# A score unit's two products issued back to back, and the fillers moved between the units

## The chip, the core and the metric

The kernel runs on one NeuronCore of a Trainium2 chip. Its engines are TensorE (PE, with its weight loads shown apart as PEld), VectorE (DVE), ScalarE (ACT), GpSimd (POOL) and SyncE (SP, which here issues nearly all DMAs). The metric is the device time of one execution in microseconds (us). Shown before: a median of 1024.78 us over 3 runs (1022.85 to 1027.67).

## What is computed

One transformer block on a sequence of S = 2048 rows of width D = 512, in fp32. Cut to the part that matters here, the attention reads:

```
q, k, v = x @ wq, x @ wk, x @ wv        # 32 heads of 16, 4 segments of 512 rows
logits = einsum("bhqd,bhkd->bhqk", qs, ks) * scale + mask     # per segment and head, causal
p      = softmax(logits, axis=-1)
a_dot  = einsum("bhqk,bhkd->bhqd", p, vs)
o      = g * a_mem + (1.0 - g) * a_dot   # a_mem: a linear memory of the earlier segments
x      = x + ga * (o @ wo)               # then layer norm, a GELU feed-forward of 1792, residual
```

The softmax needs, for each head and query row, the maximum of its 512 masked logits. Four segments times 32 heads make 128 independent 512x512 score blocks.

## The kernel before, in words

The program has three stages: projections (until about 177 us), attention (about 177 to 714 us) and the feed-forward. The change touches the attention stage alone.

**Units.** Heads are taken four at a time: Q counts 0 to 31 (a "turn" below is the work of one Q), P = 2Q and 2Q + 1 are its two pairs of heads, and h (0 or 1) is the head within a pair. The two heads of a pair lie in different halves of the array's rows, so that a product of h = 0 and one of h = 1 may run side by side. For every head there are two sorts of unit, each in three sizes:

- A score unit S (`s_unit`, products on line 622) computes logits with queries on the partitions, only to find row maxima. Size a is the block of the last 128 queries (512 keys), b the next (384), and **c holds two blocks, of 256 and of 128 keys**. The maxima are taken by a VectorE instruction on line 610 (`masked_max`), one for each block, straight from PSUM.
- A transposed unit T (`t_unit`, products on line 681) computes the logits again with keys on the partitions and the maximum already subtracted: two more rows of the stacked operands `qst` hold it. ScalarE exponentiates it into `pta`, `ptb` or `ptc` (line 684), and GpSimd zeroes what is above the diagonal (line 666).

Score units run four pairs of heads ahead of transposed ones (`LEAD`). Both take their PSUM bank from a rotation of six, `bank("att")`, so the seventh allocation has to wait until the first bank has been read.

**Fillers.** Other products stand between the units:

- Read-outs and their way back (`m_rows`, `m_put`, `m_send`): GpSimd gathers the maxima of a Q, `m_put` transposes them by one product (line 639), ScalarE copies them to `ms`, and SP writes them into two rows of `qst` for the T units of that Q.
- Value products (`pv_part`, line 702): four parts j = 0 to 3 per Q, of 512, 384, 256 and 128 columns, into the single bank `pv`, which `pv_out` copies out after the last.
- Output parts (`wo_part`, line 790): three full-width products into the bank `mm`, two such triples in a turn once the first segment is done.
- `v_last` (line 466): value projections of the last segment, done in the first turns.

**What sets the order.** The string `ORDER` lists the units of one turn, with 20 slots c0 to c19 between them. The table `PRM` gives each filler a position: `20 * Q + d` is slot d of turn Q (d of 20 or more lies in a later turn). Each engine executes what is put on it strictly in that order; semaphores that the framework derives from the tiles do the rest. It keeps a PSUM bank as a whole: a product into a bank waits for a reader of another part of it.

Of the kernel before, what the change touches and what calls it, by code (L numbers as in the profile page):

```python
# [22 lines left out]
VW = 17  # L23
VROW = 576
EPS = 1e-5
ORDER = ('Sa0 Ta1 c0 Ta0 Sa1 c1 c2 Sb0 Tb1 c3 Tb0 Sb1 c4 c5 Sc0 Tc1 c6 Tc0 Sc1 c7 '
         'Sa2 Ta3 c8 c9 Ta2 Sa3 c10 c11 Sb2 Tb3 c12 Tb2 Sb3 c13 Sc2 Tc3 c14 Tc2 Sc3 c15 c16 c17 c18 c19')
PRM = {'turn': 2,
 'pv': [[31, 0, 0, 512], [36, 1, 128, 512], [37, 2, 256, 512], [38, 3, 384, 512]],
 'pvlast': [[25, 0, 0, 512], [30, 1, 128, 512], [31, 3, 384, 512], [35, 2, 256, 512]],  # L30
 'mrows': -21,
 'mput': [-16, -15],
 'stacks': -65,
 'den': 95,
 'dnl': 18,
 'rbl': 13,
# [7 lines left out]
 'olo': 138,  # L44
 'quick': {'dnl': 11, 'den': 84, 'rbl': 12, 'mix': 107, 'ohi': 117, 'olo': 119},
 'end': {'dnl': 11, 'den': 84, 'rbl': 7, 'mix': 103, 'ohi': 111, 'olo': 116},
 'wo': [[20 * i + o for i in range(8) for o in (4, 11)]] * 2 + [[20 * i + o for i in range(4) for o in (4, 7, 11, 18)]],
 'wox': -25,
 'mixu': 12,
 'olou': 12,  # L50
# [4 lines left out]
 'wl': [26, 66, 77, 81],  # L55
 'gate': 209,
# [45 lines left out]
def block_kernel(ctx: ExitStack, tc: tile.TileContext, x, wq, wk, wv, wo, betaq, betam,  # L102
# [22 lines left out]
    def copy(e, dst, src):  # L125
        if e == "a":
            act.activation(dst, src, AF.Copy)  # L127
        else:
            (v if e == "v" else pool).tensor_copy(dst, src)
# [74 lines left out]
    with ExitStack() as pa:  # L204
# [4 lines left out]
        def pst(name):  # L209
            return pp.tile([128, 512], F32, tag="ps", name=name)  # L210
# [107 lines left out]
        ps = pst("mpsa")  # L318
# [10 lines left out]
        for ds in ((0,), (1, 2, 3)):  # L329
# [4 lines left out]
            n = slice(ds[0], ds[-1] + 1)  # L334
# [177 lines left out]
        for s in range(NSEG):  # L512
            for tok in PRM["A"][s].split():
                n = int(tok[1]) if len(tok) > 1 and tok[1].isdigit() else 0
                if tok[0] in "QKN":
                    proj(s, "k" if tok[0] == "K" else "q", n)
                elif tok[0] == "V":
                    ps = pst(f"v{s}_{n}")
# [64 lines left out]
    with ExitStack() as pb:  # L583
# [17 lines left out]
        def bank(n):  # L601
            turn[n] = turn.get(n, -1) + 1
            return banks[n][turn[n] % len(banks[n])]
# [4 lines left out]
        def masked_max(dst, src, n):  # L608
            n_dump[0] += 1
            v.tensor_tensor_reduce(out=dump[n_dump[0] % 2][:, :n], in0=src, in1=maskb[:, 512 - n:], scale=-1.0, scalar=-4 * NEG,  # L610
                                   op0=ALU.add, op1=ALU.min, accum_out=dst)

        def s_unit(P, z, h):
            Q, p = P // 2, P % 2
            if Q not in nms:
                nms[Q] = nmt[Q % len(nmt)]
            ps = bank("att")
            o = 0
            for i in ((3,), (2,), (1, 0))["abc".index(z)]:
                n = 128 * (i + 1)  # L620
                q, k = stack(qst, P, h, 48), stack(kst, P, h, 48)
                pe.matmul(ps[:, o:o + n], q[:, 128 * i:128 * i + 128], k[:, :n], start=True, stop=True)  # L622
                masked_max(nms[Q][:, h, p, i:i + 1], ps[:, o:o + n], n)
                o += n

        def stack(st, P, h, rows):
            return st[P // 2 % NK][64 * h:64 * h + rows, P % 2].bitcast(F32R)
# [7 lines left out]
            nss[Q] = r  # L635

        def m_put(Q):
            ps = bank("pv")
            pe.matmul(ps[:, :128], nss.pop(Q), identr, start=True, stop=True)
            ms = sb.tile([32, 128], F32, tag="ms", bufs=2, name=f"ms{Q}")  # L640
            copy(PRM["mse"], ms, ps[:32, :128])
            mss[Q] = ms
# [232 lines left out]
        def at(P, part, f, *a):  # L875
            todo.setdefault((P, part), []).append((f, a))
# [23 lines left out]
        def ap(pos, f, *a):  # L900
            at(pos // 10, pos % 10, f, *a)
# [8 lines left out]
        for Q in range(32):  # L910
            z = Q // 8
            pv = PRM["pv" if Q < 31 else "pvlast"]
            pvo = pv[3][0]
            ap(20 * Q + PRM["mrows"], m_rows, Q)
            put = 20 * Q + PRM["mput"][Q < 2]
            ap(put, own, "pv", ("m", Q), m_put, (Q,), True)
            ap(put + PRM["msl"], m_send, Q)
            for i, (d, j, lo, hi) in enumerate(pv):
                ap(20 * Q + d, own, "pv", Q, pv_part, (Q, j, lo, hi, i == 0, i == 3), False)
            ap(20 * Q + pvo, own, "pv", Q, pv_out, (Q,), True)  # L920
            if Q < 31:
                ap(20 * Q + pvo + PRM["tsl"], pv_store, Q)
# [60 lines left out]
        for Q in range(-LEAD // 2, NP // 2 + 1):  # L983
            for k, P in enumerate(PRM["w1at"]):
                if P // 2 == Q:
                    load_w1(k)
            for tok in ORDER.split():
                if tok[0] == "c":
                    n = int(tok[1:])
# [19 lines left out]
    with ExitStack() as pc:  # L1009
        c1 = pc.enter_context(tc.tile_pool(name="c1", bufs=1, side="right", reuse_waits="tile"))  # L1010
# [255 lines left out]
        for p in range(2):  # L1266
            n = FH * p + FH - 1
# [56 lines left out]
        for p in range(2):  # L1324
            for j in range(FH):
                quad(FH * p + j, j == 0)
            n = FH * p + FH - 1
# [73 lines left out]
```

## Time and profile before

| what | value |
|---|---|
| runs shown | 1027.67, 1024.78, 1022.85 us |
| profiled execution: its own time, its span | 1025.51 us, 1023.8 us |
| mean granted TensorE clock over the span | 0.813 |
| busy PE, DVE, ACT, POOL | 920.7, 577.9, 453.1, 279.9 us |
| granted clock from 213 to 392 us, 392 to 614 us, 614 to 695 us | 0.56, 0.62, 0.81 |

Durations in the trace are those of one execution. A busy PE is modelled: a product counts as busy until its result has drained, so consecutive products overlap in the list. The granted clock is a separate record; in the attention stage it takes the values 0.5 and 1.0 alone, for stretches of 3.41 us or a multiple. "Idle before, releaser" names what ended an engine's wait.

### The profile page before, as it was taken

The page shows a single profiled execution, that of the slowest core. Times are in us where ns is not written, and L with a number is a line of the kernel's source. Part 1 is how long each engine was busy: PE and PEld are TensorE (multiplying, and loading weights), DVE is VectorE, ACT ScalarE, POOL GpSimd, SP SyncE. Part 2 cuts the span into 40 slices and gives each one's busy share as a digit, 9 for nine tenths or more (in the row PEclk, how much of TensorE's full clock was granted, in tenths as well). Part 3 has the DMA queues.
Part 4 walks back from the last instruction along what each step waited for, and adds up shares of the span by engine and source line. Part 5 has one row for each costly group of instructions (what it writes and reads, how often), then busy time and mean ns, then how long its engine had stood idle before and what let it go on. Part 6 is the DMA issues. An engine that isn't in the chain of part 4 may idle for free.

```text
span 1023.8 us, 14348 instructions
## 1 busy us (share of the span) xinstructions
PE 920.7 (90%) x4521; PEld 600.4 (59%) x4521; DVE 577.9 (56%) x1624; ACT 453.1 (44%) x882; POOL 279.9 (27%) x503
## 2 busy tenths in 40 slices
PE   9999999878887888878887888779999999999998
PEld 5877786543333344334333344335788888888887
DVE  6676754454555554455545545558878597543243
ACT  4444445134444344343433344436667544465221
POOL 1232421022343323323332463425232003221000
PEclk9999999755565555666665658878999999999999
DMA  8957639323334345344543354743485756454543
GB/s 291 346 198 282 225 132 318 104 43 93 87 94 106 75 105 107 92 99 112 130 111 98 102 123 109 163 140 107 145 287 197 236 180 181 134 176 144 177 144 110
DMA packets 102707, 156.23 MB, mean 153 GB/s; under 512 B 15332, under 2 KB 31076, under 8 KB 102632
## 3 DMA queue, kind: packets, MB, share of 16 engines
q1 hardware_dynamic: 101768, 153.76, 50.1%
q10 hardware_dynamic: 864, 1.57, 0.4%
q8 instruction: 35, 0.57, 0.2%
q14 instruction: 40, 0.33, 0.1%
HBM read 93.95 MB, written 60.83 MB: 151 GB/s over the span
## 4 chain that ended last, share of the span: by engine, by line
PE 74%; DVE 10%; issue 9%; POOL 2%; DMA 2%; ACT 2%; SPq 0%; DVEq 0%; ACTq 0%
PE att L622 11%; PE pv L702 9%; PE bx L1048 7%; DVE dump L610 7%; PE att L681 5%; PE mm L790 5%; PE bx L1318 4%; PE q L315 4%; PE by L1318 4%; PE bv L1318 4%; PE bv L1048 4%; PE k L315 3%; PE v L466 3%; PE spare L1318 2%; PE by L1048 2%
## 5 line engine op out<-in xcount | busy, mean ns | idle before, releaser
L610 DVE CUSTOM_DVE_ANT_0 dump<-att,maskb 128x512 bf16<-128x512 f32 (+3 forms) x512 | 236.9, 489 | 246.9 <-PE att L622 130.2
L622 PE MATMUL att<-kst,qst 48*128 48x512 f32 (+3 forms) x512 | 216.4, 501 | 87.6 <-DVE nm L610 87.6
L622 PEld LDWEIGHTS att<-kst,qst 48*128 48x128 f32 x512 | 117.9, 262 | 182.2 <-DVE nm L610 121.4
L681 PE MATMUL att<-qst,kst 50*128 50x512 f32 (+3 forms) x512 | 165.9, 487 | 8.2 <-DVE nm L610 7.6
L684 ACT ACTIVATE pta<-att 128x512 f32<-128x512 f32 x128 | 69.4, 595 | 102.3 <-PE pv L702 48.5
L681 PEld LDWEIGHTS att<-qst,kst 50*128 50x128 f32 x512 | 89.0, 265 | 27.8 <-DVE nm L610 23.3
L684 ACT ACTIVATE ptc<-att 128x384 f32<-128x384 f32 x128 | 55.9, 488 | 90.6 <-PE att L681 73.8
L666 POOL TENSOR_SCALAR_AFFINE_SELECT ptc<-ptc 128x256 f32<-128x256 f32 x128 | 51.5, 413 | 95.9 <-ACT ptc L684 91.4
L666 POOL TENSOR_SCALAR_AFFINE_SELECT pta<-pta 128x256 f32<-128x256 f32 x64 | 27.5, 429 | 176.5 <-ACT pta L684 171.9
L684 ACT ACTIVATE ptb<-att 128x384 f32<-128x384 f32 x128 | 57.5, 499 | 16.8 <-PE att L681 10.5
L834 POOL TENSOR_TENSOR wb<-wa 128x256 f32<-128x256 f32 x24 | 20.2, 843 | 152.1 <-DVE hr L855 68.0
L702 PE MATMUL pv<-pta,V 128*32 128x512 f32 x248 | 56.5, 1002 | 0.0
L127 ACT ACTIVATE ts<-pv 128x512 f32<-128x512 f32 x31 | 18.6, 599 | 77.8 <-PE pv L702 72.0
L136 DVE TENSOR_TENSOR gl<-s,gh 128x512 fp32r<-128x512 f32 x34 | 24.1, 709 | 41.9 <-ACT gh L133 41.8
L702 PEld LDWEIGHTS pv<-ptc,V 128*32 128x32 f32 x496 | 24.0, 170 | 38.1 <-issue 37.6
L702 PE MATMUL pv<-ptc,V 128*32 128x256 f32 (+1 forms) x496 | 45.1, 512 | 0.0
L702 PE MATMUL pv<-ptb,V 128*32 128x384 f32 x248 | 43.4, 790 | 0.0
L610 DVE DVE_READ_ACCUMULATOR2_ANT nm<- 128x1 f32 x512 | 42.4, 83 | 0.0
L133 ACT ACTIVATE gh<-s 128x512 fp32r<-128x512 f32 x34 | 21.3, 628 | 46.6 <-PE spare L1318 17.2
L1053 ACT ACTIVATE s<-s,b1t 128x512 f32<-128x512 f32 x42 | 30.3, 721 | 21.1 <-DVE s L1057 21.1
L1057 DVE TENSOR_TENSOR s<-bv,s 128x512 f32<-128x512 f32 x28 | 19.3, 688 | 31.5 <-PE bv L1048 21.9
L666 POOL TENSOR_SCALAR_AFFINE_SELECT ptb<-ptb 128x256 f32<-128x256 f32 x64 | 26.2, 409 | 38.1 <-ACT ptb L684 38.0
(363 smaller groups left out, 2083.1 us busy)
## 6 DMA issues: line engine op xcount, KB each, us to landing
GD<-s SPq DMA_DIRECT2D x56, 256.0 KB
s<-GD SPq DMA_DIRECT2D x52, 256.0 KB
kst<-KD SPq DMA_DIRECT2D x64, 192.0 KB
qst<-QD SPq DMA_DIRECT2D x64, 192.0 KB
QD<-q SPq DMA_DIRECT2D x16, 512.0 KB
KD<-k SPq DMA_DIRECT2D x16, 512.0 KB
TD<-ts SPq DMA_DIRECT2D x32, 256.0 KB
xt<-X2D SPq DMA_DIRECT2D x28, 256.0 KB
```

Source lines behind the costliest of these rows:

```text
L315: pe.matmul(ps, a[:, k, 128 * g:128 * g + 128], b[k], start=(k == 0 and i == 0), stop=(k == KB - 1 and i == 2))
L466: pe.matmul(ps, a[k][:, 128 * b:128 * b + 128], w[:, k, :], start=(k == 0 and i == 0), stop=(k == KB - 1 and i == 2))
L610: v.tensor_tensor_reduce(out=dump[n_dump[0] % 2][:, :n], in0=src, in1=maskb[:, 512 - n:], scale=-1.0, scalar=-4 * NEG, op0=ALU.add, op1=AL ...
L622: pe.matmul(ps[:, o:o + n], q[:, 128 * i:128 * i + 128], k[:, :n], start=True, stop=True)
L666: pool.affine_select(out=t, in_=t, pattern=pattern, compare_op=ALU.is_ge, fill=0.0, base=0, channel_multiplier=-1)
L681: pe.matmul(ps[:, o:o + n], k[:, 128 * j:128 * j + 128], q[:, 128 * j:], start=True, stop=True)
L684: act.activation(pt[:, h, :], ps[:, :m], AF.Exp, scale=0.25)
L702: pe.matmul(ps[32 * c:32 * c + 32, lo:hi], V[4 * s + j][:, VW * hd:VW * hd + 32], pt[:, c % 2, lo - o:hi - o], start=start, stop=stop)
L790: pe.matmul(ps, a[:, 128 * b:128 * b + 128], w[:, g, :], start=(g == 0 and i == 0), stop=(g == 3 and i == 2))
L1048: pe.matmul(ps, a[:, i, k, :], b[k], start=start and k == 0 and c == 0, stop=k == 1 and c == 2, skip_group_check=not start)
L1053: act.activation(dst, src, AF.Gelu_apprx_tanh, bias=b1t[:, f:f + 1])
L1318: pe.matmul(ps, a[:, c], w[:, lo:hi], start=(f == 0 and i == 0), stop=(last and i == 2))
```

## The change

Three things change, all in the attention stage.

1. In `s_unit`, the products of a unit are issued first, and then its maxima. Only size c has more than one.
2. `m_put` takes its bank from the rotation of six rather than the `pv` bank, and its slot goes from 4 (5 for the first two Q) to 6 of the turn.
3. Positions: the four value products of a Q go from 31, 36, 37 and 38 to 21, 27, 30 and 35; an output triple goes from slot 11 to slot 13 (the last segment here: 4, 7, 11, 18 to 4, 9, 13, 17); the stack loads go from -65 to -63; the sixteen steps of `v_last` get even distances. In `ORDER` slot c8 now stands ahead of Sa2, c14 ahead of Sc2, and c16 between Tc3 and Tc2.

```diff
-ORDER = ('Sa0 Ta1 c0 Ta0 Sa1 c1 c2 Sb0 Tb1 c3 Tb0 Sb1 c4 c5 Sc0 Tc1 c6 Tc0 Sc1 c7 '
-         'Sa2 Ta3 c8 c9 Ta2 Sa3 c10 c11 Sb2 Tb3 c12 Tb2 Sb3 c13 Sc2 Tc3 c14 Tc2 Sc3 c15 c16 c17 c18 c19')
+ORDER = ('Sa0 Ta1 c0 Ta0 Sa1 c1 c2 Sb0 Tb1 c3 Tb0 Sb1 c4 c5 Sc0 Tc1 c6 Tc0 Sc1 c7 c8 '
+         'Sa2 Ta3 c9 Ta2 Sa3 c10 c11 Sb2 Tb3 c12 Tb2 Sb3 c13 c14 Sc2 Tc3 c15 c16 Tc2 Sc3 c17 c18 c19')
- 'pv': [[31, 0, 0, 512], [36, 1, 128, 512], [37, 2, 256, 512], [38, 3, 384, 512]],
+ 'pv': [[21, 0, 0, 512], [27, 1, 128, 512], [30, 2, 256, 512], [35, 3, 384, 512]],
- 'mput': [-16, -15],
- 'stacks': -65,
+ 'mput': [-14, -14],
+ 'stacks': -63,
- 'wo': [[20 * i + o for i in range(8) for o in (4, 11)]] * 2 + [[20 * i + o for i in range(4) for o in (4, 7, 11, 18)]],
+ 'wo': [[20 * i + o for i in range(8) for o in (4, 13)]] * 2 + [[20 * i + o for i in range(4) for o in (4, 9, 13, 17)]],
- 'vl': [[-39, -36, -39, -36], [-31, -31, -27, -23], [-19, -18, -19, -18], [-9, -9, -4, -1]],
+ 'vl': [[-39, -37, -36, -34], [-33, -31, -29, -28], [-26, -24, -22, -20], [-18, -13, -8, -3]],
...
-            o = 0
+            o, parts = 0, []
             for i in ((3,), (2,), (1, 0))["abc".index(z)]:
                 n = 128 * (i + 1)
                 q, k = stack(qst, P, h, 48), stack(kst, P, h, 48)
                 pe.matmul(ps[:, o:o + n], q[:, 128 * i:128 * i + 128], k[:, :n], start=True, stop=True)
+                parts.append((i, o, n))
+                o += n
+            for i, o, n in parts:
                 masked_max(nms[Q][:, h, p, i:i + 1], ps[:, o:o + n], n)
-                o += n
...
-            ps = bank("pv")
+            ps = bank("att")
...
-            ap(put, own, "pv", ("m", Q), m_put, (Q,), True)
+            ap(put, m_put, Q)
```

On PE before, the c units of a turn's second pair of heads and what follows them. `att_1912` to `att_1917` are the six banks of the rotation, `kst` and `qst` the stacked operands, and the brackets name the engines on whose semaphores a product waits.

```order
L622 MATMUL att_1917<-kst_1924,qst_1923 128x256 [waits Activation_49]
L622 MATMUL att_1917<-kst_1924,qst_1923 128x128 [waits DVE_49]
L681 MATMUL att_1912<-qst_1703,kst_1704 128x128
L681 MATMUL att_1912<-qst_1703,kst_1704 128x256
L681 MATMUL att_1913<-qst_1703,kst_1704 128x128
L681 MATMUL att_1913<-qst_1703,kst_1704 128x256
L622 MATMUL att_1914<-kst_1924,qst_1923 128x256 [waits Activation_49]
L622 MATMUL att_1914<-kst_1924,qst_1923 128x128 [waits DVE_49]
L702 MATMUL pv_1918<-ptb_3761,V_200 32x384 x2
L702 MATMUL pv_1918<-ptb_3815,V_200 32x384 x2
L702 MATMUL pv_1918<-ptc_3781,V_201 32x256 x2
```

And now the c units of a turn's first pair, where `m_put` has moved to (line numbers from 639 on are two higher):

```order
L622 MATMUL att_1916<-kst_1924,qst_1923 128x256 [waits Activation_49]
L622 MATMUL att_1916<-kst_1924,qst_1923 128x128
L683 MATMUL att_1917<-qst_1703,kst_1704 128x128 [waits DVE_49]
L683 MATMUL att_1917<-qst_1703,kst_1704 128x256
L641 MATMUL att_1912<-identr,nmr_1905 128x128 [waits DVE_49,Pool_49]
L683 MATMUL att_1913<-qst_1703,kst_1704 128x128 [waits Activation_49]
L683 MATMUL att_1913<-qst_1703,kst_1704 128x256
L622 MATMUL att_1914<-kst_1924,qst_1923 128x256 [waits Activation_49]
L622 MATMUL att_1914<-kst_1924,qst_1923 128x128
L704 MATMUL pv_1918<-ptb_3765,V_200 32x384 x2
L704 MATMUL pv_1918<-ptb_3820,V_200 32x384 x2
L622 MATMUL att_1915<-kst_1924,qst_1923 128x512 [waits DVE_49]
```

The product of 128 columns no longer waits for VectorE; `m_put` stands among the T products, with a bank of the rotation; and one part of the value products follows a pair, where all of three parts followed the turn's second pair before.

On SP's queue, where one Q's stacks are loaded, before (`dn`, `opk` and `amB` are the loads of the finished value products and of the memory's part; `X2D` is the block's result so far):

```order
L757 DMA rbB_4289<-RD_4213 128x1x512
L177 DMA kst_1992<-KD_3_100 48x2x512 x2
L177 DMA qst_1991<-QD_3_84 48x2x512 x2
L725 DMA dn_4339<-TD_4108 128x1x32
L727 DMA opk_4341<-TD_4108 128x1x512
L734 DMA amB_4343<-AMD_0_113 128x512
```

and now:

```order
L759 DMA rbB_4292<-RD_4215 128x1x512
L727 DMA dn_4318<-TD_4096 128x1x32
L729 DMA opk_4320<-TD_4096 128x1x512
L736 DMA amB_4322<-AMD_0_113 128x512
L177 DMA kst_2001<-KD_3_100 48x2x512 x2
L177 DMA qst_2000<-QD_3_84 48x2x512 x2
```

In every other turn the three loads stand ahead of the stack loads instead of behind them.

## The prediction

> **What bounds the kernel now.** First the page's slices of the clock, then busy time by stage with the waits of each stage, then the order of time within a turn, and last the clock.
>
> ```profile
> PEclk9999999755565555666665658878999999999999
> ...
> 177.00:213.00 36.00, 29.89 (x89) 18.05 (x87) 17.15 (x75) 8.68 (x13) 1.00 (x5) 0.68 0.32 99
> 213.00:392.30 179.30, 147.09 (x750) 71.16 (x748) 94.14 (x391) 77.80 (x175) 60.17 (x134) 0.56 0.39 91
> 392.30:613.83 221.53, 180.23 (x925) 87.62 (x923) 111.08 (x444) 86.02 (x191) 82.37 (x158) 0.62 0.44 108
> 613.83:694.56 80.73, 64.46 (x382) 31.01 (x380) 41.98 (x174) 34.56 (x76) 27.84 (x58) 0.81 0.52 136
> ...
> 213.00:392.30 179.30, 4.96 (x12) 2.94 (x12) 0.56 0.39 91
> 392.30:613.83 221.53, 4.56 (x13) 2.63 (x13) 0.62 0.44 108
> 613.83:694.56 80.73, 1.65 (x6) 0.94 (x6) 0.81 0.52 136
> ```
>
> The first four rows of stretches give PE, PEld, DVE, ACT and POOL busy, then clock, DMA share and GB/s; the last three give line 639 alone. TensorE is the busiest engine throughout, but only in attention is it neither full (147 of 179 us) nor at full clock (0.56). The stretches are cut at products of line 639, one for each Q: they hold 12, 13 and 5 turns (the last row counts the product on either cut), so a turn lasts 14.9, 17.0 and 16.1 us. I call them B, C and D, and the first one A.
>
> What PE waits for, in the whole span and then in A, B, C and D:
>
> ```profile
> PE att L622 <- DVE nm L610: 87.6, 128, 1.6
> PE att L681 <- DVE nm L610: 7.6, 23, 0.5
> ...
> PE att L622 <- DVE nm L610: 6.1, 8, 1.3
> ...
> PE att L622 <- DVE nm L610: 29.0, 48, 0.9
> PE att L681 <- DVE nm L610: 2.6, 7, 0.5
> ...
> PE att L622 <- DVE nm L610: 37.7, 52, 1.6
> PE att L681 <- DVE nm L610: 3.9, 14, 0.5
> ...
> PE att L622 <- DVE nm L610: 14.8, 20, 1.2
> PE att L681 <- DVE nm L610: 1.7, 4, 0.5
> ```
>
> PE's idle time is this and nothing else: 179.30 - 147.09 = 32.2 us in B against 31.6 us of listed waits, 41.3 against 41.6 in C, 16.3 against 16.5 in D. There are 128 waits on line 622, one for each c unit. Where they sit, in order of time:
>
> ```profile
> 410.18 0.38 PE L622 MATMUL att<-kst,qst 48*128 48x256 f32 x1
> 411.09 0.32 PE L622 MATMUL att<-kst,qst 48*128 48x128 f32 x1 [0.53 <-DVE nm L610]
> ...
> 412.25 0.80 PE L622 MATMUL att<-kst,qst 48*128 48x128 f32 x2 [0.55 <-DVE nm L610]
> 412.52 0.95 PE L681 MATMUL att<-qst,kst 50*128 50x512 f32 x2
> 413.06 0.63 PE L622 MATMUL att<-kst,qst 48*128 48x512 f32 x1
> 413.62 1.94 PE L702 MATMUL pv<-pta,V 128*32 128x512 f32 x8
> 415.48 0.80 PE L790 MATMUL mm<-woh,oh 128*128 128x512 f32 x1
> 416.08 0.63 PE L790 MATMUL mm<-woh,ol 128*128 128x512 f32 x1
> 416.50 0.63 PE L790 MATMUL mm<-wol,oh 128*128 128x512 f32 x1
> 417.06 0.69 PE L622 MATMUL att<-kst,qst 48*128 48x384 f32 x1
> ```
>
> The 256-column product goes out, its maximum is taken, and only then follows the 128-column product into the other part of the same bank. So DVE, busy for about half of the time, holds up PE four times a turn.
>
> The clock, in the records' own stretches of 3.41 us (PE busy, clock, DMA):
>
> ```profile
> 398.06:401.47 3.41, 3.41 (x12) 0.50 0.00 0
> 401.47:404.88 3.41, 1.91 (x11) 0.50 0.11 15
> 404.88:408.30 3.42, 3.42 (x30) 0.50 1.06 231
> 408.30:411.71 3.41, 2.62 (x17) 1.00 0.56 152
> 411.71:415.12 3.41, 2.87 (x13) 0.50 0.24 79
> ...
> 613.10:616.51 3.41, 2.69 (x18) 1.00 0.44 135
> 616.51:619.92 3.41, 2.87 (x21) 1.00 0.48 110
> 619.92:623.34 3.42, 2.23 (x16) 1.00 0.38 132
> ```
>
> A full stretch at half clock is followed by one at full clock (404.88, then 408.30); a fast stretch with waits in it loses the clock (2.62 of 3.41 busy, then 0.50), one with a little more work keeps it (2.69 and 2.87, and the next is still 1.00). A full stretch is not always enough: 398.06 was full, and 401.47 still ran at 0.50. The Trainium skill (TensorE: Matmul & The Clock Gate, "The HAM clock gate") has the clock rise after one busy window of about 3.4 us and fall only after an idle one, and advises against idle gaps over about 3 us. By that rule attention would hold the full clock already, and the change would earn its waits alone, some 938 us; the trace disagrees, since no wait exceeds 1.6 us and the clock still falls to 0.50 at 411.71, so this gets no chance of its own.
>
> **The change part by part.**
>
> *Both products first.* The 128 waits of 87.6 us lose their cause. A c unit's first maximum now waits for both products. DVE has the room: 94.14 of 179.30 us busy in B, 111.08 of 221.53 in C.
>
> *What the clock makes of it.* PE's work in full-clock time is (stretch - waits) x clock, taking the waits as spread evenly: B (179.3 - 31.6) x 0.56 = 82.7 us, 6.9 a turn; C (221.5 - 41.6) x 0.62 = 111.5, 8.6 a turn; D (80.7 - 16.5) x 0.81 = 52.0, 10.4 a turn (it also turns the layer norm's rows). One turn of the trace ran near this already:
>
> ```profile
> 645.49:659.19 13.70, 10.43 (x73) 5.08 (x71) 7.37 (x33) 7.07 (x17) 8.47 (x14) 0.88 0.63 134
> ...
> PE att L622 <- DVE nm L610: 2.8, 4, 1.2
> PE att L681 <- DVE nm L610: 0.9, 2, 0.5
> ```
>
> 13.70 us at clock 0.88 with 3.7 us of waits leave 10.0 us of work, 8.8 at full clock, close to C's 8.6. Without waits more stretches are full, so more are followed by fast ones, and fast ones keep their clock. I take 0.75 in B, where the S and T products with their 48 and 50 rows are a larger part, and 0.90 in C and D, which have the full-width triples. Bounds: 1.0 everywhere, and 0.5 everywhere, for 398.06 shows that full is not always enough.
>
> *What waits remain.* DVE has 94.14 / 12 = 7.8 us a turn in B and 8.5 in C, ACT 6.5 and 6.6; against PE's 8.6 none of them is far off, and six banks hold half a pair's units. The remaining waits, a bank whose reader is late, I put at 1.6 us a turn in B and 1.4 in C and D, half of today's 2.6 to 3.3. Bounds: 0.4, and today's amount.
>
> *Fillers spread.* Going from the half-height products to another shape and back costs: the first full-width product takes 0.60 us to the next one's start (415.48 to 416.08), the second 0.42 (416.08 to 416.50), the last 0.56 to the S product (417.06). That is 0.15 us an edge at half clock. Three value parts that stood in one row, and `m_put`, which stood beside a triple, become excursions of their own: some six more edges a turn, 0.9 us at half clock, 0.45 at full. Against it stands what the listed waits leave out: a product after a wait starts after the drain of the one before it. A full-width product lists 0.63 us (416.08), yet the next follows after 0.42, so 0.2 us of it is drain; four times that is 0.8 us a turn at half clock. I set both to cancel, plus or minus 0.4 us a turn, 12 us in all. The Trainium skill (TensorEngine Tiling (Array Packing), "Key Properties") says that a change of tiling mode drains the engine, which speaks against spreading; the 0.15 us edges agree. Without the cancelling it would add 30 x 0.45, about 14 us.
>
> *Earlier value products* free `pta` sooner. In the row below ACT waited for it ten times from 300 to 600 us; that wait goes. It lies beside PE's work, so I count nothing for it, and nothing would be lost if PE outran ACT.
>
> ```profile
> ACT pta L684 <- PE pv L702: 31.5, 10, 3.2
> ...
> SPq L177 <- PE att L622: 145.8, 18, 9.8
> ```
>
> *`m_put` in the rotation* makes 25 allocations a turn of six banks; the units behind it find a bank read five units ago rather than six. It waits for POOL's two read-out steps, with the T products queued behind it on PE. Seven slots lie between, 7/20 of a turn: 3.8 us at 11 us a turn. POOL is 34 to 37% busy, so I count nothing; a POOL backlog would cost its length each turn (rival 3).
>
> *DMAs.* Stack loads move past three loads in every other turn. SP waits 145.8 / 18 = 8.1 us a turn for the stack to be free, so these stand ready in front of it. From slot 17 the S units that need the stack come 23 slots later, 12.6 us at 11 us a turn. C's DMA share of 0.44 would become 0.44 x 17.0 / 11.0 = 0.68, and 404.88 shows that bursts pass that. Nothing counted. The DVE pair of `den` now stands between two c maxima every other turn; it lies in the 1.4 to 1.6 us.
>
> **The sum**, against the profiled execution's 1025.5 us:
>
> - B: 6.9 / 0.75 + 1.6 = 10.8 us a turn, 12 turns, 129.6 for 179.3: -49.7
> - C: 8.6 / 0.90 + 1.4 = 11.0, 13 turns, 143.0 for 221.5: -78.5
> - D: 10.4 / 0.90 + 1.4 = 13.0, 5 turns, 65.0 for 80.7: -15.7
> - A: its 6.1 us of waits, less some rest: -5
>
> Together -149: 876.5 us. The median of the runs lies 0.7 us below the profiled execution, so **876 us**. The lower end: clock 1.0 and 0.4 us of waits, but no turn under DVE's 7.8 in B, gives 8.2, 9.0 and 10.8 us: -81, -105, -27, -6, so 807. The upper end of this theory, clock 0.65 and 0.8 with the same waits: 12.2, 12.2 and 14.4 a turn: -33, -63, -9, -4, so 917.
>
> **Rivals.**
>
> 1. *The waits go, the clock stays* at 0.56, 0.62 and 0.81, as the spread leaves each stretch with its mean. For it: 398.06. Against it: C's fast stretches lost the clock exactly where c units waited. With 0.6 us of waits left: 6.9 / 0.56 + 0.6 = 12.9, 8.6 / 0.62 + 0.6 = 14.5, 10.4 / 0.81 + 0.6 = 13.4; -24, -33, -14, -5: 949 us.
> 2. *All stretches equally dense, none dense enough*: **slower**. Today's fast stretches follow the value products that stand in a row (404.88). If spread products keep every stretch just under what raises the clock, it stays at 0.5: 13.8 + 0.5 = 14.3 in B, 17.2 + 0.5 = 17.7 in C, 20.8 + 0.5 = 21.3 in D; -8, +9, +26, A -5: 1047 us. It decides as soon as C's clock falls under 8.6 / (17.0 - 0.5) = 0.52. Against it: all stretches would have to miss the level, while today's, with their gaps, reach it for the 12% (B) and 24% (C) of the time that clocks of 0.56 and 0.62 mean.
> 3. *Another engine's chain sets the turn*: `m_put` behind POOL, or late loads, with PE waiting for them. For it: POOL had 8.47 us in the turn at 645.49. Two to three us a turn on top of 11.0 give about 13.5: 162, 175.5 and 67.5; -17, -46, -13, -5: 944 us.
> 4. *It does not do what it says*: the second product still waits, for the bank's earlier reader. The order shows no wait on it, so little is left of this: 1020 us.
>
> **How the numbers follow.** Forecast 0.58, rival 1 0.20, rival 3 0.13, rival 2 0.06, rival 4 0.03. The forecast's own range is 825 to 917; to leave out no more than 2 in 10, the range must take in rivals 1 and 3: **825 to 962**. Runs of this kernel differ by some 0.5%, which is what can be told from no change. Faster by more than that: 0.92; within it 0.02; slower 0.06.
>
> **What would show it.** Right: the row "PE att L622 <- DVE nm" falls from 87.6 us to under 45, with none of it ahead of a 128-column product; the clock from 213 us on reads 0.7 or more and 0.85 or more in the turns with triples; the products of line 641, one for each Q, lie about 11 us apart. Rival 1: the waits fall but the clock reads 0.55 to 0.65. Rival 2: the clock reads 0.5 and PE is full. Rival 3: the product of line 641 or the first S products of a stack wait for POOL or a DMA. I would be wrong in the main step if PE's idle time per turn stayed near 3 us under another name.

## The result, and the profile after

| | before | after |
|---|---|---|
| median of 4 runs each, us | 1025.69 (1022.85 to 1027.67) | 840.73 (832.39 to 845.69) |
| ratio | | 0.8137, 95% interval 0.8088 to 0.8186 |
| profiled execution, its span, us | 1025.51, 1023.8 | 832.39, 830.7 |
| mean granted clock over the span | 0.813 | 0.955 |

The change takes 185 us away, almost a fifth of the time. Ratios, here and below, leave out the executions that ran at a lower clock (845.69 and 845.01 us of after's four), while medians hold them all, so the two differ by some us. The profiled execution of after is the fastest of its four; where stages are compared below, it is with this execution. The page's slices of the clock, after:

```profile
PEclk9999999999997697899996999999999999999999
```

Before, the attention slices read 5 to 8; now they read 6 to 9. By stage, cut at the `m_put` products (line 641 now) of the same four Q as before, the columns as in the prediction: length, then PE, PEld, DVE, ACT and POOL busy, clock, DMA share, GB/s. The last row is all thirty turns:

```profile
202.60:311.14 108.54, 101.11 (x759) 48.68 (x760) 86.12 (x394) 77.23 (x174) 59.93 (x135) 0.83 0.60 146
311.14:442.66 131.52, 125.47 (x929) 59.98 (x927) 102.60 (x447) 88.28 (x192) 80.47 (x156) 0.94 0.72 186
442.66:503.16 60.50, 59.03 (x374) 27.99 (x374) 40.95 (x169) 35.76 (x75) 28.95 (x61) 0.83 0.62 177
202.60:503.16 300.56, 285.61 (x2060) 136.66 (x2060) 229.68 (x1010) 201.27 (x441) 169.36 (x351) 0.88 0.66 170
```

A turn takes 9.0, 10.1 and 12.1 us in B, C and D, where it took 14.9, 17.0 and 16.1. The same thirty turns before, in one row, and then PE's waits after, over the whole span:

```profile
213.00:694.56 481.56, 391.78 (x2053) 189.79 (x2051) 247.20 (x1007) 198.38 (x440) 170.39 (x349) 0.63 0.43 106
```

```profile
PE att L683 <- DVE nm L610: 5.4, 7, 1.7
PE att L683 <- DMA qst<-ms: 3.5, 4, 2.3
PE att L641 <- POOL nmr L636: 2.8, 3, 1.3
PE att L641 <- DVE nm L610: 2.0, 7, 0.3
```

Line 622 is no longer in the list. PE's idle time in the thirty turns fell from 481.56 - 391.78 = 89.8 us to 300.56 - 285.61 = 15.0. That accounts for 75 of the 181 us which these turns lost; the other 106 us are the clock, 0.63 before and 0.88 now. So the larger part of the gain is not the waits themselves.

The clock still falls in places. Stretches of the records after, with PE busy, clock, DMA share and GB/s, the last row for the seven stretches between; then the wait that ended at 259.28:

```profile
254.98:258.39 3.41, 2.57 (x29) 1.00 0.45 133
258.39:261.80 3.41, 2.52 (x11) 0.50 0.99 222
...
285.70:289.11 3.41, 3.08 (x33) 1.00 0.81 183
...
261.80:285.70 23.90, 23.89 (x136) 0.50 0.41 101
```

```profile
259.28 0.90 PE L683 MATMUL att<-qst,kst 50*128 50x512 f32 x2 [1.73 <-DVE nm L610]
```

A fast stretch that was busy for only 2.57 of 3.41 us is followed by one at 0.50, in which the wait of 1.73 us ends. Seven full stretches, 23.89 of 23.90 us busy, follow at 0.50 before the clock comes back at 285.70.

The view puts this wait down to VectorE, but the maximum that ends just then is that of the score unit ahead, which has another bank of the rotation. The rows that the product needs are on their way at this time. SP issued their two copies at 253.45:

```profile
253.45 1.39 SPq L651 DMA_DIRECT2D qst<-ms  x2
```

By the trace's record of landings the second came in at 259.14, 0.14 us ahead of the product. All six waits of more than half a microsecond on line 683 end 0.13 or 0.14 us behind such a landing. They make 7.8 of the 8.9 us of the first two rows of waits, so after the change the T units wait for these rows far more than for banks. From 210 us on the clock falls four more times in the thirty turns, each time around another wait of over 1 us (ending at 241.01, 318.26, 442.66 and 476.54).

### The profile page after: what moved, and what is told of

Its sections match the earlier page's. It is cut to its first block, busy times and chain, and to the rows that moved or that the text cites. A ratio compares the mean times of both kernels' runs of the same rounds, so it can differ in the third digit from the quotient of the medians.

```text
span 830.7 us, 14390 instructions
## 1 busy us (share of the span) xinstructions
PE 808.6 (97%) x4521; PEld 541.5 (65%) x4521; DVE 559.9 (67%) x1624; ACT 455.8 (55%) x882; POOL 278.6 (34%) x503
## 4 chain that ended last, share of the span: by engine, by line
PE 41%; POOL 4%; DMA 2%; DVE 2%; ACT 1%; issue 1%; SPq 0%; DVEq 0%; POOLq 0%; ACTq 0%
PE bx L1050 8%; PE bx L1320 5%; PE by L1320 5%; PE bv L1320 5%; PE bv L1050 4%; PE spare L1320 2%; PE by L1050 2%; PE pv L704 2%; PE mm L792 2%; PE mm L1320 2%; PE att L683 2%; PE att L622 1%; POOL xt L567 1%; DMA qst<-ms 1%; POOL ptc L668 1%
## 5 line engine op out<-in xcount | busy, mean ns | idle before, releaser
L610 DVE CUSTOM_DVE_ANT_0 dump<-att,maskb 128x512 bf16<-128x512 f32 (+3 forms) x512 | 225.9, 488 | 74.7 <-PE att L622 26.1
L683 PE MATMUL att<-qst,kst 50*128 50x512 f32 (+3 forms) x512 | 157.2, 407 | 9.2 <-DVE nm L610 5.4
L622 PE MATMUL att<-kst,qst 48*128 48x512 f32 (+3 forms) x512 | 151.7, 386 | 0.0
L622 PEld LDWEIGHTS att<-kst,qst 48*128 48x128 f32 x512 | 85.4, 205 | 88.7 <-ACT pta L686 36.8
L686 ACT ACTIVATE ptc<-att 128x384 f32<-128x384 f32 x128 | 63.0, 493 | 31.8 <-PE att L683 30.4
L704 PE MATMUL pv<-pta,V 128*32 128x512 f32 x248 | 40.3, 718 | 1.0 <-ACT ts L127 1.0
L1059 DVE TENSOR_TENSOR s<-bv,s 128x512 f32<-128x512 f32 x28 | 19.3, 689 | 30.7 <-PE bv L1050 21.2
L704 PE MATMUL pv<-ptc,V 128*32 128x256 f32 (+1 forms) x496 | 35.7, 362 | 0.0
L501 POOL TENSOR_SCALAR qp<-qp 128x512 f32<-128x512 f32 x12 | 18.5, 1541 | 42.2 <-ACT qp L496 42.2
L704 PE MATMUL pv<-ptb,V 128*32 128x384 f32 x248 | 29.0, 543 | 0.0
L136 DVE TENSOR_TENSOR w1ml<-s,w1mh 128x512 fp32r<-128x512 f32 x18 | 13.0, 721 | 21.8 <-ACT w1mh L133 21.8
```

Of the source, the lines that this page charges most:

```text
L136: lo_eng.tensor_tensor(out=lo, in0=src, in1=hi.bitcast(F32), op=ALU.subtract)
L683: pe.matmul(ps[:, o:o + n], k[:, 128 * j:128 * j + 128], q[:, 128 * j:], start=True, stop=True)
L686: act.activation(pt[:, h, :], ps[:, :m], AF.Exp, scale=0.25)
L704: pe.matmul(ps[32 * c:32 * c + 32, lo:hi], V[4 * s + j][:, VW * hd:VW * hd + 32], pt[:, c % 2, lo - o:hi - o], start=start, stop=stop)
```

## The experiments

Each run's ratio is to the kernel before on the same chip, with its 95% interval. Edits are against the changed kernel unless another is named; one that begins with "And" stands on the run told before it. "Work" below is PE's busy time by the clock, (length - idle) x clock. It is no fixed quantity: B's turns read 7.0 us in after at 0.83, and 6.2 in a run below at 0.50 (148.99 x 0.50 / 12). So only stretches of like clock are compared by it.

### Which half of the change does it

**The products first, and nothing else** (against the kernel before):

```diff
-            o = 0
+            o, parts = 0, []
...
-                masked_max(nms[Q][:, h, p, i:i + 1], ps[:, o:o + n], n)
+                parts.append((i, o, n))
                 o += n
+            for i, o, n in parts:
+                masked_max(nms[Q][:, h, p, i:i + 1], ps[:, o:o + n], n)
```

> Kernel before with the two products of a c unit issued first, and nothing else: read-outs stay in the pv bank, value products stay in their two rows. Theory (the waits ahead of the 128-column products held the clock down; spreading the fillers lets VectorE and ScalarE catch up while TensorE does value products): the waits on line 622 ahead of the 128-column product go, but after each row of value products the units run into banks not yet read, so 0.8 to 1.5 us of waits a turn return on lines 622 and 681; the clock from 213 us on reads 0.7 to 0.9; 880 to 930 us. Rival 1 (the first edit does it all, the spread is worth nothing): within 1.5% of the changed kernel, 830 to 850 us, clock near 0.9 in attention. Rival 2 (only spread fillers let the clock hold): clock stays near 0.6, 940 to 965 us.

Measured: 859.5 us, 0.8421 (0.8356 to 0.8487), below the theory's range and above rival 1's. The thirty turns, and PE's waits:

```profile
196.19:527.57 331.38, 302.68 (x2052) 153.04 (x2051) 234.30 (x1008) 197.31 (x440) 169.17 (x349) 0.78 0.61 151
```

```profile
PE att L683 <- DVE nm L610: 22.1, 54, 1.7
PE pv L641 <- POOL nmr L636: 5.4, 3, 2.5
```

This edit alone gives about 165 of the 185 us. What stays is 22.1 us of T units that find their bank not yet read, against 7.6 of that kind before.

**The spread, and nothing else** (the old `s_unit` put back into the changed kernel):

```diff
-                parts.append((i, o, n))
+                masked_max(nms[Q][:, h, p, i:i + 1], ps[:, o:o + n], n)
                 o += n
-            for i, o, n in parts:
-                masked_max(nms[Q][:, h, p, i:i + 1], ps[:, o:o + n], n)
```

> Changed kernel with the old s_unit: each maximum is taken before the next product of its unit, everything else as changed. Theory: 128 waits of 0.5 to 0.7 us are back, four a turn, and every 3.41 us stretch of a turn without output triples holds one or two of them, so its clock falls for long; turns with triples hold it in part. Clock 0.6 to 0.7 from 213 to 392 us of the old count, 0.75 to 0.9 later; 930 to 980 us. Rival 1 (the waits cost only their own length): 841 + 128 x 0.55 = 911 us with the clock near that of the changed kernel. Rival 2 (the spread is worth nothing): as before, 1010 to 1030 us.

Measured: **1066.4 us, 1.0418 (1.0352 to 1.0485), slower than before**; every expectation missed, and the nearest is rival 2. The four rows are B, C, D and all thirty turns:

```profile
222.97:415.63 192.66, 155.94 (x760) 70.86 (x760) 91.45 (x393) 82.10 (x174) 60.67 (x134) 0.55 0.35 88
415.63:633.45 217.82, 188.79 (x928) 83.69 (x928) 108.85 (x444) 89.78 (x191) 82.00 (x157) 0.67 0.42 108
633.45:729.46 96.01, 85.39 (x374) 38.45 (x373) 44.97 (x173) 37.01 (x76) 29.46 (x59) 0.61 0.39 115
222.97:729.46 506.49, 430.12 (x2060) 193.00 (x2059) 245.26 (x1008) 208.89 (x441) 172.13 (x350) 0.61 0.39 102
```

```profile
PE att L622 <- DVE nm L610: 82.8, 128, 1.3
```

The 128 waits are all there. At a like clock (0.61 and 0.63) the work is 430.12 x 0.61 = 262 us against 391.78 x 0.63 = 247: the spread adds 15 us at full clock, about 25 at 0.61. And D's clock fell from 0.81 to 0.61. So the spread alone costs 43 us (1023.27 to 1066.4, both on one chip), and on top of the first edit it gains 859.5 - 840.7 = 19 by the medians, 29 by the ratios (0.8421 to 0.8137). The two parts do not add up.

### Do waits cost their length?

**Old order for one head of each pair**, so that two of a turn's four waits stay:

```diff
-                parts.append((i, o, n))
+                if h:
+                    masked_max(nms[Q][:, h, p, i:i + 1], ps[:, o:o + n], n)
+                else:
+                    parts.append((i, o, n))
```

> Changed kernel with the old order of product and maximum in the c units of h = 1 alone: two waits a turn in place of none or four. Theory (the clock tips at a level of work per 3.41 us stretch; two waits leave most stretches above it): about 64 x 0.5 = 32 us of waits and some more cold stretches, 870 to 900 us, clock 0.85 or more in attention. Rival (the clock falls in proportion to the waits, no level): half way between the changed kernel and the run with the spread alone. Rival (waits hidden by the banks filled ahead): under 850 us.

Measured: 932.13 us (922.22 to 968.55), 0.9022 (0.8947 to 0.9097). The theory's 870 to 900 us missed. The half-way rival is nearer, but its point, (0.8137 + 1.0418) / 2 = 0.928, lies outside the interval too. From the profile of a 941.05 us execution, B, then one of its turns (PE busy, clock, DMA share and GB/s), and PE's wait:

```profile
208.35:370.84 162.49, 148.99 (x760) 70.39 (x760) 89.28 (x394) 80.16 (x174) 60.53 (x135) 0.50 0.44 105
```

```profile
246.25:259.94 13.69, 12.57 (x65) 0.50 0.50 114
```

```profile
PE att L622 <- DVE nm L610: 39.3, 63, 1.4
```

39.3 us of waits make the kernel 91 us slower than after. The rest of the difference is the clock: all of B runs at 0.50 in this execution, and in the two shortest, which have no profile, the mean over the span is 0.88 where after has 0.95. A turn of 13.69 us is close to four stretches of the clock (13.65 us), which led to a theory: a turn that fills a whole number of stretches shows each of them the same work every time, and if none is dense enough, the clock is locked.

**The same with 24 idle triples more** in the first twelve turns (72 full-width products into the bank `mm`, whose results nothing reads):

```diff
+        def extra():
+            for i in range(3):
+                pe.matmul(mm, maskb[:, :128], maskb, start=True, stop=True)
+
+        for t in range(12):
+            for o in (4, 13):
+                ap(20 * t + o, extra)
```

> The run with half the waits, and in its first twelve turns (which have no output triples) two triples of full-width products each, at slots 4 and 13, into a bank that nothing reads: 72 products more than needed. In the run with half the waits these turns ran at clock 0.50 throughout, 13.65 us each, with TensorE waiting 13.5 us in 162. Theory (the clock goes by the work done in each 3.41 us stretch, and those turns lie just under the level): the added work lifts the clock to 0.65 to 0.8, the turns become 11.5 to 13.5 us long, and the whole 910 to 935 us, no slower than without the added work (932). Rival (the clock goes by waits alone, the work is simply added): 24 triples of 1.3 to 1.6 us at half clock, 31 to 38 us more, 963 to 970 us.

Four executions took 997.87, 892.98, 989.75 and 903.16 us, so no median speaks for it, and neither range holds one of them. Two are 19 us and more *below* the shortest execution of the kernel without the extra work (922.22). The profile is of the slowest. A second run of the same program, on another chip, gave one of a faster execution:

> The same program as the run with 24 dummy triples, once more, for a profile of its fast executions (893 and 903 us; only one of the slow ones, 997.87 us, left a trace, with turns of 17.04 us, five clock stretches of 3.41 us, at 0.50). Theory: the turn locks to a whole number of clock stretches while TensorE runs at half clock, so each stretch of each turn has the same mix of work and none rises. Then a fast execution has its first twelve turns at a clock of 0.85 or more, of 10 to 12 us each, and their lengths are no multiple of 3.41; if it is slow again, they read 17.04 once more. Rival: the two times come from something else than these turns (the later stages, or a lower clock throughout); then a fast execution has the same 17 us turns at 0.50 in this stretch and its time is saved elsewhere.

Executions of 934.55 (profiled) and 976.45 us. Turns of both profiles, with PE busy, clock, DMA share and GB/s; first that of 997.87 us, one turn and eleven together, then five of the turns of that of 934.55:

```profile
242.29:259.34 17.05, 15.59 (x71) 0.50 0.33 78
...
225.25:412.90 187.65, 171.66 (x771) 0.50 0.35 85
```

```profile
236.75:246.96 10.21, 9.09 (x74) 1.00 0.54 131
246.96:257.18 10.22, 9.10 (x74) 1.00 0.64 153
257.18:269.28 12.10, 10.67 (x73) 0.86 0.63 149
...
300.26:310.81 10.55, 9.12 (x73) 1.00 0.46 113
310.81:321.04 10.23, 9.11 (x73) 1.00 0.57 149
```

This is one program, with 38.7 and 40.7 us of waits on line 622 in all. One execution does these turns in 17.05 us at 0.50, the other in 10.2 at 1.00. The slow turn is idle for 1.46 of 17.05 us, 9%, and doesn't gain the clock; the fast one is idle for 1.12 of 10.21, 11%, and keeps it, or gets it back within a turn (257.18). The stretches of the records show how both can last. Five stretches of the slow execution, then three of the fast one (PE busy, clock, DMA share and GB/s):

```profile
242.42:245.84 3.42, 2.86 (x13) 0.50 0.02 5
245.84:249.25 3.41, 3.22 (x20) 0.50 0.00 0
249.25:252.66 3.41, 3.10 (x17) 0.50 0.00 0
252.66:256.08 3.42, 3.03 (x13) 0.50 0.77 159
256.08:259.49 3.41, 3.41 (x16) 0.50 0.85 226
...
231.06:234.47 3.41, 2.85 (x26) 1.00 0.21 65
234.47:237.89 3.42, 3.03 (x23) 1.00 1.05 195
237.89:241.30 3.41, 3.24 (x27) 1.00 0.36 131
```

Much the same busy times, 2.85 to 3.24 us, keep the full clock where it is and do not bring it back where it is lost. All fourteen profiles agree, stretch by stretch, from the first change of the clock after 195 us until 500 us (until 700 us in the kernel before and the one with the spread alone). At 0.50, none of the 173 stretches that were busy for less than 89% was followed by one at 1.00, and of the 325 full ones 126 were. At 1.00, all 46 that were busy for less than 68% were followed by a fall, none of the 353 that were busy for 97% or more, and 80 of the 349 between. So the clock is lost by a stretch with long waits and comes back, as a rule, only after a full one. Why most full ones do not bring it back, the runs don't show.

My expectation was half right. The fast turns are at full clock and 10 to 12 us long, but 10.2 us is close to three stretches (10.24), so a whole number of stretches does not by itself hold the clock down. What lifts one execution and not the other stays open: the fast one, too, ran at 0.50 until 231 us.

The Trainium skill (TensorE: Matmul & The Clock Gate, "A second HAM failure mode: psum-queue depth-cycling") tells of a kernel in which short idle times of PE between groups of products made the clock swing between two levels. The kernel before agrees, with waits of no more than 1.6 us. The Trainium skill (TensorE: Matmul & The Clock Gate, "The HAM clock gate") has the clock return after one busy window of about 3.4 us; after's trace differs, with full stretches from 261.80 to 285.70 at 0.50.

### What in the spread gains

**Three of the four value parts in one slot**, the first left where it is:

```diff
- 'pv': [[21, 0, 0, 512], [27, 1, 128, 512], [30, 2, 256, 512], [35, 3, 384, 512]],
+ 'pv': [[21, 0, 0, 512], [35, 1, 128, 512], [35, 2, 256, 512], [35, 3, 384, 512]],
```

> Changed kernel with the last three value products of a Q in one row again (slots 21, 35, 35, 35 in place of 21, 27, 30, 35). Theory (spread fillers give VectorE and ScalarE time to empty the banks, so that no wait over half a microsecond is left to tip the clock): bank waits of 0.5 to 0.9 us come back once a turn, clock in attention 0.8 or less, 848 to 862 us. Rival (the spread only costs shape changes, four edges of 0.08 to 0.15 us a turn): 825 to 838 us.

Measured: 836.9 us, 0.8174 (0.8127 to 0.8221): no different from after, as the rival had it. The theory, that the even distances matter, missed.

**The first part moved as well**, from between a turn's a and b units to behind its c units:

```diff
- 'pv': [[21, 0, 0, 512], [27, 1, 128, 512], [30, 2, 256, 512], [35, 3, 384, 512]],
+ 'pv': [[27, 0, 0, 512], [35, 1, 128, 512], [35, 2, 256, 512], [35, 3, 384, 512]],
```

> Changed kernel with the four value products of a Q at slots 27, 35, 35 and 35: three in a row as in the run before, and the first after the c units, so that no value product stands between the a and the b units. With products first alone, the second T unit of size b waited 0.85 us a turn for the maximum of an a unit, and nothing stood between a and b there in the first half of a turn. Theory (what counts is a filler between the a and b units, not that the value parts stand apart): these waits return once or twice a turn, clock in attention 0.75 to 0.82, 850 to 870 us. Rival (the place of the value products is worth nothing, the gain over products first alone comes from m_put leaving the pv bank and from the stack loads): 833 to 845 us.

Measured: 876.71 us, 0.8569 (0.8508 to 0.863), a little more than the theory's range.

```profile
201.00:541.07 340.07, 313.82 (x2051) 157.45 (x2051) 227.72 (x1009) 200.28 (x441) 169.24 (x350) 0.80 0.59 150
```

```profile
PE att L683 <- DVE nm L610: 10.5, 31, 1.2
PE att L622 <- ACT ptc L686: 8.8, 18, 0.7
...
291.97 0.44 PE L622 MATMUL att<-kst,qst 48*128 48x384 f32 x1 [0.72 <-ACT ptc L686]
```

The last two kernels differ in one entry of the table, 21 or 27, and in 40 us. With the 512-column part between the a and the b units, VectorE and ScalarE have its time to empty the banks that the b units need; the last row is such a b unit without it. Without it units wait for their banks 49 times, 19.3 us in all, and the clock of the thirty turns is 0.80, not 0.86 as in the kernel before it. Losing this one place costs more than the whole spread had gained, and even distances earn nothing. What the bank of `m_put`, the stack loads and the triple's new slot are worth was not run apart, nor was this part's old place, slot 11, between the a and b units of the turn's second pair.

### Can the waits that are left go too

**`m_send` from ScalarE's queue** rather than SP's, straight behind the copy that it needs:

```diff
-            mss[Q] = ms
+            for h in range(2):
+                act.dma_start(qst[Q % NK][64 * h + 48:64 * h + 50], ms[16 * h:16 * h + 16])
...
-            ap(put + PRM["msl"], m_send, Q)
```

> Changed kernel with the read-out's two small DMAs (qst<-ms) issued from ScalarE's queue right after the copy, not from SP's queue behind the stack loads. In the profile of the changed kernel the clock fell at 241, 258 and 320 us right after T products had waited 1.5 to 2.3 us for these rows, and stayed at 0.5 for 3, 27 and 17 us. Theory (a single wait of over 1 us tips the clock, and the turns after it run half as fast although TensorE has no wait): these three falls go, 15 to 25 us less, 810 to 825 us by the profiled run, and the spread of the runs shrinks. Rival 1 (the issue takes ScalarE 0.6 us each, two a turn, and ScalarE becomes the one that is waited for): same or slower, 835 to 860 us, with waits for ACT on line 622. Rival 2 (the small rows land late because the DMA engines are full, whatever the queue): same time, the same T waits.

Measured: 825.18 us, 0.8052 (0.7992 to 0.8112); profiled 826.98, a little over the theory's upper edge. The medians put it 16 us below after, the ratios 9, and the two intervals overlap, so a gain is likely, but its size is not shown. After's waits of SP's queue have a row that fits:

```profile
SPq L651 <- ACT ptc L686: 46.8, 22, 5.2
```

On SP's queue the two small copies of a Q hold up everything behind them until ScalarE has done its work up to the copy into `ms`. The waits for the rows became fewer but did not go (4.7 us, 4 times, for the six of 7.8 us in after), and the clock of the thirty turns is 0.92. The Trainium skill (DMA: Bandwidth & Descriptors, "Issuing engines are not separate DMA queues") says that issuing from several engines saves only the issue time. The row above suggests more than that here: loads no longer held up behind the copies. That is argued and not shown apart.

**And the layer norm of the first segment on VectorE** instead of GpSimd, whose long step stood ahead of `m_put`'s read-out:

```diff
-                ap(ln["on"][b], ln2_apply, i, b, (pool, v)[i])
+                ap(ln["on"][b], ln2_apply, i, b, v)
```

> The kernel of the run with the send from ScalarE's queue, and the layer norm of the first segment (line 567, four operations of 2.08 us each on GpSimd) moved to VectorE. In that run the product of m_put waited 1.24 us for GpSimd at 409.7 us and the clock stayed at 0.5 for 13.7 us. Theory (one wait over 1 us tips the clock): that fall goes, about 7 us less, 815 to 820 us. Rival (VectorE, at 85% of a fast turn, becomes late): the same or slower by 3 to 8 us, with waits for line 610 in those turns.

Measured: 819.37 us (815.59 to 839.39), 0.7973 (0.7943 to 0.8003), in the theory's range. The interval overlaps with that of the run before, and the one profile is of the execution of 839.39 us, so it is not shown that the fall is gone.

**And `v_last` at its old positions** (that line of the change undone):

```diff
- 'vl': [[-39, -37, -36, -34], [-33, -31, -29, -28], [-26, -24, -22, -20], [-18, -13, -8, -3]],
+ 'vl': [[-39, -36, -39, -36], [-31, -31, -27, -23], [-19, -18, -19, -18], [-9, -9, -4, -1]],
```

> As the run before in this list, with the sixteen last value projections (v_last) at their old positions. The first T product stood at 194.1 us with products first alone and at 198 to 200 us in the kernels with the new positions. Theory (in the first turns the even distances cost shape changes and hide nothing, since VectorE is not late there): 2 to 5 us less than the run before. Rival: no difference beyond 3 us, the earlier start being due to m_put alone.

Measured: **815.71 us, 0.7929 (0.7885 to 0.7972), the fastest of all**, 25 us below after by the medians and 21 by the ratios, with intervals apart. The three edits together are thus a gain; the 4 us of the last one alone lie within the spread of the runs. The slices of the clock, and the thirty turns:

```profile
PEclk9999999999799989999999999999999999999999
```

```profile
197.26:479.40 282.14, 273.43 (x2059) 132.87 (x2059) 231.55 (x1014) 193.87 (x441) 162.50 (x347) 0.95 0.71 182
```

A turn takes 9.4 us. PE is idle for 8.7 us and at 0.95 of full clock, so not much is left here for waits to give.

**And the read-out's steps on VectorE** rather than GpSimd:

```diff
-            pool.tensor_copy(hl[:, :, 0], n)
-            pool.tensor_tensor(out=hl[:, :, 1], in0=n, in1=hl[:, :, 0].bitcast(F32), op=ALU.subtract)
+            v.tensor_copy(hl[:, :, 0], n)
+            v.tensor_tensor(out=hl[:, :, 1], in0=n, in1=hl[:, :, 0].bitcast(F32), op=ALU.subtract)
```

> The kernel with the send from ScalarE's queue, the layer norm on VectorE and the old positions of v_last, and the two steps that gather the maxima (lines 633 and 634 of before) moved from GpSimd to VectorE. The product of m_put waits 0.3 us in most fast turns and 0.6 to 1.2 us where GpSimd is behind. Theory (these waits start falls of the clock): waits on m_put go below 0.2 us, 805 to 813 us, smaller spread of the runs. Rival (VectorE has 7.0 of the 7.5 us of a fast turn without triples and gets 0.2 to 0.4 more): same or up to 6 us slower.

Measured: 830.46 us, 0.8097 (0.8047 to 0.8148), 15 us worse: the rival's direction, and more.

```profile
PE att L684 <- DVE nm L610: 7.7, 8, 1.7
```

The wait for GpSimd is gone, but eight waits for VectorE now take 7.7 us (2.9 before this step). That these make the 15 us is not shown: the next kernel has more of them.

**And `m_put` one slot earlier**, as the rows are now ready sooner:

```diff
- 'mput': [-14, -14],
+ 'mput': [-15, -15],
```

> As the run before in this list, with m_put one slot earlier (5 in place of 6), so that the rows leave about 0.5 us earlier for the T units. Theory (T products that wait for the rows start falls): fewer of these waits, 0 to 5 us less than the run before. Rival (m_put then waits for VectorE's last maximum instead, 0.3 to 0.5 us each turn): 0 to 8 us more.

Measured: 823.98 us, 0.803 (0.7975 to 0.8085): 6.5 us less, with overlapping intervals, and still behind the fastest. In its profile the waits for VectorE are 14, of 11.8 us, yet the mean clock over the span is 0.981 where the run before has 0.958.

## Why the prediction was right, and where not

The forecast of 876 us lies 35 us above the median, and its range holds it. The mechanism was right: without the waits the clock rises. The step that failed is **the term for the waits left**. Against the profiled execution, the forecast of 876.5 is 44 us too high: 21.1 in B, 11.5 in C, 4.5 in D, and 7 outside.

- *The bound.* Right: the 128 waits left the list, and with them no idle time came up under another name.
- *Work a turn.* PE busy by the clock is 101.11 x 0.83 / 12 = 7.0 us in B, 125.47 x 0.94 / 13 = 9.1 in C, 59.03 x 0.83 / 5 = 9.8 in D, for 6.9, 8.6 and 10.4. In sum 251 us for 246: right.
- *The clock.* 0.83, 0.94 and 0.83 for 0.75, 0.90 and 0.90. B was better than forecast and is worth 12 x (6.9 / 0.75 - 7.0 / 0.83), some 9 us; D missed the 0.85 that was named as the mark.
- *Waits left.* Forecast 1.6 us a turn in B and 1.4 in C and D, "half of today's". By idle time it is 0.6, 0.5 and 0.3, which makes 11.8 + 12.1 + 5.5, about 29 of the 44 us. The halving came from no row, and the term was for banks whose reader is late, while most of what is left are waits for the rows of maxima (7.8 us in six waits) and for `m_put`'s input. DVE's and ACT's busy time a turn, from which I argued that they were "not far off", says how full an engine is, not how late it is: in B, DVE is now 86.12 of 108.54 us busy and PE hardly waits for it. The run with the products alone has 28.7 us of idle time, 1.0 a turn, still under the forecast.
- *The spread against the drain.* The forecast was +14 us of work against some 12 saved. The spread alone gave +15. The products alone gave 236 us (302.68 x 0.78) for 247, so -11, though at a higher clock, where the same turns read more. The first size is right, and the second as far as unlike clocks can be compared. The Trainium skill (TensorEngine Tiling (Array Packing), "Key Properties") has a change of tiling mode drain the engine; the 15 us agree, though no run parts this cost from the others of the spread.
- *Nothing counted for where the fillers stand.* Wrong: they move the waits. The first value part between the a and b units is worth 40 us (836.9 to 876.71). The forecast could not tell these two places apart; of the kernel with the worse one it would have looked exact, by luck.
- *Earlier value products.* ACT's wait for `pta`, 31.5 us from 300 to 600 us before, is no longer among its waits there; that it earns nothing by itself agrees with the run that moves three of the parts back for no change.
- *`m_put` and DMAs, counted at nothing.* `m_put` waits for POOL three times, 2.8 us. The way of the rows from `m_put` back to the T units was not counted at all: it is what the six longest waits of the T units end with, and moving its copies off SP's queue gave 9 to 16 us less, with overlapping intervals. Rival 3 named these places, at 2 to 3 us a turn; they come to a fraction of that. Its sum is also too low in D, where 13.5 us a turn is hardly over the forecast's own 13.0; with 15.5 it would come to some 954 us.
- *Rivals.* 1 fell (0.88 for its 0.63), but in D the clock did stay, 0.83 for 0.81. 2 did not come about in after, yet the spread with the waits kept is slower than before, by 43 us, with C's clock at 0.67, above the 0.52 I gave as the point of turning: B and D turned, not C. 4 fell.

What stays open: what decides whether a full stretch raises the clock. Busy time alone does not (full at 0.50, from 261.80 on), nor does a whole number of stretches (10.2 us at 1.00).

## What to carry to other kernels

Where dependencies on a PSUM bank are kept for the bank as a whole, issue all products into it before its first reader; a reader in between becomes a wait of PE in every unit. Price short waits of TensorE by what they do to the clock, not by their length: here 39 us of them cost 91. The full clock is easier kept than regained, so the waits to remove first are those that leave a stretch well under full. Put a filler where the engines that empty the banks need time, rather than at even distances, and look at what stands behind a waiting DMA on its queue.

## What was not expected of the hardware

- The clock has two levels that tend to last. One program did the same turns in 17.05 us at 0.50 and in 10.2 us at 1.00, with 9% and 11% idle time, over eleven turns and eight. In the attention stage of all profiles no stretch at 0.50 that was busy for less than 89% was followed by the full clock (173 of them), while of the stretches at full clock that were busy for 68 to 97% 269 of 349 kept it.
- More work can take less time: with 72 products added, two of six executions took 893 and 903 us, where the four without them took 922 to 969. The other four took 935 to 998.
- Full is not enough: in after's trace TensorE was busy throughout seven stretches in a row, from 261.80 to 285.70, and stayed at 0.50 until their end.
- A copy of 8 KB can hold up TensorE: in after's trace six T products waited 0.6 to 2.3 us for such copies to land; one of these landed 5.0 us after its issue (254.18 to 259.14). Issuing the 64 copies from ScalarE's queue rather than SP's went with 9 to 16 us less, with overlapping intervals.
